# Linear attention, 2048 x 640: value weights in ten transfers instead of fifteen, and a shorter list of final waits

## The chip, the cores and the metric

The kernel runs on one core of a Trainium2 chip. The metric is device time in microseconds (us) for one execution. Before the change three runs took 100.31, 100.75 and 101.52 us; the median is 100.75 us. A separate execution was profiled; its lines are what is read here.

## The reference

One sequence of 2048 rows and 640 features goes through a linear-attention block with 32 heads of width 20, and then through an output projection:

```
qkv = x @ wqkv                      # x: 2048 x 640, wqkv: 640 x 1920
q, k, v = split into 32 heads of 20
phi(t) = where(t > 0, t + 1, exp(t)) + 1e-6
kv  = sum over s of phi(k)[s] (x) v[s]        # 20 x 20 per head
z   = sum over s of phi(k)[s]
o   = (phi(q) @ kv) / (phi(q) . z + 1e-6)
out = o @ wo                        # wo: 640 x 640
```

All inputs and the output are bf16.

## The kernel before, in words

The kernel never forms v. It uses that the sum over rows of phi(k) times v is (phi(k)^T x) times the value part of wqkv. So TensorE first makes phi(k) (`k_half` L288, `k_phi` L302), then P = x^T phi(k), accumulated over 16 row tiles (`state_mm` L316, used by `p_step` L324 and `p_block` L679). From P and the value weights `wv` it makes the small kv blocks (`kv_group` L439, its matmuls are L445), masks them to the heads (`kv_mask` L454), multiplies them with `wo` (`w2_four` L505, `w2_two` L525, whose matmuls are L472) and moves the result into `w2p` by small DMAs (`w2_move`, L494). In between it makes phi(q) transposed (`q_tile` L348, matmuls L354), the denominators (`den` L538, matmuls L544), spreads their reciprocals over the partitions by DMA (`den_spread`, L561) and scales phi(q) with them (`normalize`, L569). Last come the 16 output tiles: `out_mm` (L576) into PSUM, `out_evac` (L599 on ScalarE, L602 on VectorE) into one of four SBUF buffers `osb`, and a store by `out_dma` (L587).

All work is put down in a small plan. `Plan.add` (L36) appends an operation to its engine's list and works out which semaphore values it has to wait for; `Plan.emit` (L78) writes each list out with its waits. The order is written out by hand: the loads first, then a string of letters (L722), one letter per step. Every engine runs its list in order, and so does each DMA queue owner: SyncE (SP) issues nearly all transfers, so a transfer that must wait holds up those behind it.

`Plan.known[eng]` (L30) holds, for each engine, the semaphore values that its list has certainly seen at that point. Each operation carries a `clock`, a copy of what its engine knew when it was added (L69). When an engine waits for an operation, it takes over that operation's clock too (L57 to L59). So an engine can know that a transfer has landed without having waited for that transfer's own semaphore: it is enough that it waited for an operation of another engine which had waited for it. `add` leaves out waits that are already known (L54). The final loop (L730 to L732) does not look at `known`: it makes SP wait for each of the 17 output stores.

The loads stand on SP's queue in this order: part of x and of the key weights (`load_wk`, L235), five transposing loads of x (`load_xT`, L187), and then `load_rest` (L258): the query weights `wqn` (L224), three pieces of x in its own layout `xn` (L230), the value weights `wv` (L266), and `wo` as `wog` (L273, L277). After `load_rest`, SP's list goes on with the two transposes of the z sums (`z_turn`, L423), the moves into `w2p`, the spreading of the reciprocals and the stores.

The value weights are cut into six groups of heads: five of 120 columns and one of 40. In SBUF a 120-column group is stored as two chunks of 60 in slots of 64, with the gaps zeroed by a VectorE memset (L160), for which the first of the `wv` transfers waits. `load_rest` loads them for each of the five 128-row blocks d of wqkv. Groups 0 to 3 are one transfer per block (eight chunks of 60 elements, 120 bytes each, per partition), group 4 another (two chunks of 60) and group 5 a third (one chunk of 40): fifteen transfers. Each transfer has its own semaphore. `kv_group(0)` (letter k in the string) needs groups 0 to 3; `kv_group(1)` (letter K) needs groups 4 and 5.

The output stores use the four `osb` buffers in turn. The evacuation of tile t + 4 writes the buffer that the store of tile t reads, so ScalarE or VectorE waits for that store before it writes. Tiles 0 to 14 have one store each on SP; the last tile has two, one on SP (columns 0 to 479) and one on ScalarE's queue (columns 480 to 639), in `out_last` (L612).

Of the kernel before, what the change touches and what calls it, by code (L numbers as in the profile page):

```python
# [84 lines left out]
def bass_standalone__linear_attn_block__prompt_kernel(nc, x, wqkv, wo, out):  # L85
# [15 lines left out]
    with contextlib.ExitStack() as ctx:  # L101
# [38 lines left out]
        P = Plan(nc, es)  # L140
# [82 lines left out]
        def w_cols(dst, lo, hi, col, key, eng):  # L223
            P.add(eng, lambda e: e.dma_start(  # L224
                dst[:, 0:NC_ * D].rearrange("p (c n) -> p c n", n=D)[:, :, lo:hi],
                wqkv[:, col + lo:col + hi].rearrange("(c p) n -> p c n", p=128)),
                writes=[key], dma=True)

        def load_xn(a, b, eng):
            P.add(eng, lambda e: e.dma_start(  # L230
                xn[:, a * D:b * D].rearrange("p (t n) -> p t n", n=D),
                x[0, 128 * a:128 * b, :].rearrange("(t p) n -> p t n", p=128)),
                writes=[("xn", t) for t in range(a, b)], dma=True)
# [24 lines left out]
        def load_rest():  # L258
            w_cols(wqn, 0, D, 0, "wqn", "sp")
            for a, b in ((2, 8), (8, 12), (12, 16)):  # L260
                load_xn(a, b, "sp")
            for g, n in ((0, 4), (4, 1), (5, 1)):
                f = min(GT, gsz[g])
                k = gsz[g] // f * n
                for d in range(NC_):
                    P.add("sp", lambda e, g=g, f=f, k=k, d=d: e.dma_start(  # L266
                        wv[:, 128 * NG * d:128 * NG * (d + 1)].rearrange(
                            "p (j f) -> p j f", f=64)[:, 2 * g:2 * g + k, 0:f],
                        wqkv[128 * d:128 * (d + 1), 2 * D + goff[g]:2 * D + goff[g] + k * f].rearrange(
                            "p (j f) -> p j f", f=f)),  # L270
                        writes=[("wv", i, d) for i in range(g, g + n)], dma=True)
            for t in range(2):
                P.add("sp", lambda e, t=t: e.dma_start(  # L273
                    wog[64 * t:64 * t + GT, 0:5 * D].rearrange("p (g n) -> p g n", n=D),
                    wo[0:5 * GW, :].rearrange("(g t p) n -> t p g n", t=2, p=GT)[t]),
                    writes=[("wog", g, t) for g in range(5)], dma=True)
            P.add("sp", lambda e: e.dma_start(  # L277
                wog[0:gsz[5], 5 * D:6 * D], wo[goff[5]:, :]),
                writes=[("wog", 5, 0)], dma=True)
# [342 lines left out]
        load_wk()  # L622
        load_xT()
        load_rest()
        warm(5)
        warm(1, 128)
# [102 lines left out]
            P.emit(name, eng)  # L729
        for key in out_keys:  # L730
            op = P.writers[key]
            nc.sync.wait_ge(P.sem_obj[op.sem], op.val)  # L732


# [26 lines left out]
```

## Time and profile before

| what | value |
| --- | --- |
| median of 3 runs | 100.75 us (100.31 to 101.52) |
| the profiled execution's own time | 100.58 us |
| its span, first to last instruction | 99.3 us |
| TensorE matmul busy | 95.1 us, 96% of the span |
| VectorE, ScalarE, GpSimd busy | 63.7, 48.8, 4.7 us |
| granted TensorE clock | 1.000 |
| HBM read and written | 5.90 MB and 2.62 MB |
| issues of `wv` on SP | 15, from 18.5 us to 33.9 us |

How to read it: the span runs from the first to the last instruction that the profiler saw; the execution's own time lies 1.28 us above it. In a group line, "128x320 x170" is the shape and the count, then the busy time in us and the mean of one in ns. "SPq" is the work of SyncE as the issuer of DMAs: the duration of such a row is the time that the issue held SyncE, not the time that the data took; the time to landing is listed apart. A wait line reads "who waited <- whom: us in total, times, longest". In a timeline line the first number is the start, the second the length, both in us.

### The profile page before, as it was taken

Reading aid. Unit: us, or ns where it says so; the run is one execution under the profiler, and the core shown is the slowest. Engines: PE = TensorE matmul, PEld = TensorE weight load, DVE = VectorE, ACT = ScalarE, POOL = GpSimd, SP = SyncE. Lnnn points to the kernel's source line nnn. Section 1 sums busy time; section 2 is a strip of 40 time slices with the busy share of each in tenths; the row PEclk is TensorE's granted clock in tenths of the full one; section 3 lists DMA queues with packets and bytes.
Section 4 is the critical chain, followed back from the end, with each engine's and each line's share of the span. In section 5 each row is a group of like instructions: output and inputs, shape, how many; then the busy total and the mean of one; then the engine's idle time right before and its main releaser. Section 6 shows DMA issues by size and latency. Waiting matters only on the chain.

```text
span 99.3 us, 1827 instructions
## 1 busy us (share of the span) xinstructions
PE 95.1 (96%) x699; PEld 60.8 (61%) x699; DVE 63.7 (64%) x124; ACT 48.8 (49%) x93; POOL 4.7 (5%) x19
## 2 busy tenths in 40 slices
PE   6999999999999999999999999999999999999980
PEld 2457777777755544455678767655556677777760
DVE  5304998898899349989649836759899033551140
ACT  5116455554427020015706648796987665454430
POOL 6400000000000000000000700000000000000000
PEclk9999999999999999999999999999999999999999
DMA  2999989999996169000340023223101257233332
GB/s 60 293 256 245 231 120 119 355 362 361 308 155 91 21 134 196 5 0 0 73 66 7 0 75 99 80 49 88 52 0 51 81 110 240 92 131 132 132 125 77
DMA packets 26448, 12.60 MB, mean 127 GB/s; under 512 B 18632, under 2 KB 26440, under 8 KB 26440
## 3 DMA queue, kind: packets, MB, share of 16 engines
q1 hardware_dynamic: 25720, 11.87, 50.4%
q10 hardware_dynamic: 720, 0.61, 1.9%
q8 instruction: 5, 0.08, 0.3%
q14 instruction: 3, 0.02, 0.1%
HBM read 5.90 MB, written 2.62 MB: 86 GB/s over the span
## 4 chain that ended last, share of the span: by engine, by line
PE 91%; DMA 4%; ACT 1%; ACTq 0%; issue 0%
PE ps L576 22%; PE ps L317 22%; PE ps L354 22%; PE ps L293 22%; DMA wk<-in_wqkv_dram 4%; PE ps L445 1%; PE ps L544 1%; PE ps L472 1%; ACTq L230 0%; ACT L239 0%; ACT osb L599 0%
## 5 line engine op out<-in xcount | busy, mean ns | idle before, releaser
L317 PE MATMUL ps<-pk,xn 128*128 128x480 bf16 (+1 forms) x160 | 23.2, 300 | 0.0
L354 PE MATMUL ps<-xT,wqn 128*128 128x512 bf16 x100 | 23.1, 379 | 0.0
L293 PE MATMUL ps<-wk,xT 128*128 128x320 bf16 x160 | 22.4, 299 | 0.5 <-DMA wk<-in_wqkv_dram 0.2
L576 PE MATMUL ps<-w2p,pq 128*128 128x320 bf16 (+2 forms) x170 | 22.1, 292 | 0.0
L293 PEld LDWEIGHTS ps<-wk,xT 128*128 128x128 bf16 x160 | 15.5, 98 | 7.4 <-DMA wk<-in_wqkv_dram 1.3
L576 PEld LDWEIGHTS ps<-w2p,pq 128*128 128x128 bf16 x170 | 15.9, 98 | 6.3 <-issue 0.2
L317 PEld LDWEIGHTS ps<-pk,xn 128*128 128x128 bf16 x160 | 13.6, 98 | 9.4 <-issue 0.3
L362 ACT ACTIVATE eq<-ps 128x512 bf16<-128x512 f32 x20 | 11.9, 597 | 13.8 <-PE ps L354 13.6
L354 PEld LDWEIGHTS ps<-xT,wqn 128*128 128x128 bf16 x100 | 11.4, 118 | 9.1 <-issue 0.3
L306 ACT ACTIVATE ek<-ps 128x640 bf16<-128x640 f32 x16 | 11.2, 704 | 11.1 <-PE ps L293 10.4
L599 ACT CAST osb<-ps 128x320 bf16<-128x320 f32 (+2 forms) x27 | 11.0, 412 | 9.7 <-PE ps L576 9.0
L311 DVE SCALAR_TENSOR_TENSOR pk<-ps,ek 128x640 bf16<-128x640 f32 x16 | 13.2, 824 | 0.5
L569 DVE TENSOR_TENSOR pq<-pq,rd 128x512 bf16<-128x512 bf16 x20 | 7.3, 418 | 4.3 <-DMA rd<-rdc 4.3
L375 DVE TENSOR_SCALAR eq<-eq 128x512 bf16<-128x512 bf16 x20 | 5.7, 287 | 5.9 <-ACT eq L362 5.8
L602 DVE CAST osb<-ps 128x320 bf16<-128x320 f32 (+1 forms) x7 | 3.2, 457 | 8.7 <-PE ps L576 8.7
L308 DVE TENSOR_SCALAR ek<-ek 128x640 bf16<-128x640 bf16 x16 | 5.2, 324 | 5.4 <-ACT ek L306 5.2
L366 ACT ACTIVATE rq<-ps 128x512 bf16<-128x512 f32 x13 | 7.7, 592 | 0.0
L339 ACT CAST pt<-ps 128x480 bf16<-128x480 f32 x4 | 2.3, 563 | 8.2 <-PE ps L317 8.1
L379 DVE TENSOR_TENSOR pq<-eq,rq 128x512 bf16<-128x512 bf16 x13 | 5.5, 425 | 1.1 <-ACT rq L366 0.7
L388 DVE TENSOR_TENSOR za<-pk 128x1280 f32<-128x1280 bf16 x4 | 5.8, 1483 | 0.0
L382 DVE SCALAR_TENSOR_TENSOR pq<-ps,eq 128x512 bf16<-128x512 f32 x7 | 4.8, 692 | 0.2
L388 DVE TENSOR_TENSOR za<-za 128x1280 f32<-128x1280 f32 x3 | 4.4, 1488 | 0.0
(37 smaller groups left out, 36.2 us busy)
## 6 DMA issues: line engine op xcount, KB each, us to landing
out_dram<-osb SPq DMA_DIRECT2D x15, 160.0 KB, 1.8
xn<-in_x_dram SPq DMA_DIRECT2D x2, 640.0 KB, 8.9
xn<-in_x_dram SPq DMA_DIRECT2D x1, 960.0 KB, 7.1
wqn<-in_wqkv_dram SPq DMA_DIRECT2D x1, 800.0 KB, 5.6
wog<-in_wo_dram SPq DMA_DIRECT2D x2, 375.0 KB, 5.3
w2p<-w2g SPq DMA_DIRECT2D x10, 75.0 KB
wv<-in_wqkv_dram SPq DMA_DIRECT2D x5, 120.0 KB, 5.5
rd<-rdc SPq DMA_DIRECT2D x8, 64.0 KB, 2.2
```

Of the source, the lines that this page charges most:

```text
L293: r = e.matmul(bank(b + h, HALF), xT[:, c * S + 128 * st:c * S + 128 * st + 128], wk[:, c * D + HALF * h:c * D + HALF * (h + 1)], start=(c ...
L306: P.add("act", lambda e: e.activation(fold(t[:, :]), two_banks(b), ACTF.Exp), reads=banks + ["table"], writes=[("ek", st % 3)])
L311: P.add("dve", lambda e: e.scalar_tensor_tensor(fold(pk[:, st * D:(st + 1) * D]), two_banks(b), 0.0, fold(t[:, :]), ALU.max, ALU.add), rea ...
L317: return e.matmul(bank(d // PB[h], PW[h], off=PW[h] * (d % PB[h])), xn[:, st * D + 128 * d:st * D + 128 * d + 128], pk[:, st * D + PO[h]:s ...
L354: r = e.matmul(bank(b), wqn[:, d * D:(d + 1) * D].rearrange("p (q c) -> p c q", c=NC_)[:, c, :], xT[:, d * S + BK * sbk:d * S + BK * (sbk ...
L362: P.add("act", lambda e: e.activation(t[:, :], bank(b), ACTF.Exp), reads=[("bank", b), "table"], writes=[("eq", i)])
L366: P.add("act", lambda e: e.activation(r[:, :], bank(b), ACTF.Relu), reads=[("bank", b), "table"], writes=[("rq", i)])
L375: P.add("dve", lambda e: e.tensor_scalar(t[:, :], t[:, :], 1.0, 1e-6, ALU.min, ALU.add), reads=[("eq", i)], writes=[("eq", i)])
L388: P.add("dve", lambda e: e.tensor_tensor(d_ap, a, b, ALU.add), reads=ra + rb, writes=[dst])
L569: P.add("dve", lambda e: e.tensor_tensor(v, v, rd[i][:, BK * h:BK * (h + 1)], ALU.mult), reads=[("rd", i, 2 * h), ("rd", i, 2 * h + 1), (" ...
L576: r = e.matmul(bank(b, hi - lo), pq[:, c * S + 128 * st:c * S + 128 * st + 128], w2p[:, c * D + lo:c * D + hi], start=(c == 0), stop=(c == ...
L599: P.add("act", lambda e: e.copy(osb[j][:, lo:hi], bank(b, hi - lo)), reads=[("bank", b)], writes=keys)
```

## The change

Two edits. In `load_rest`, groups 0 to 3 and group 4 become one transfer per block, of ten chunks of 60 elements per partition; group 5 stays as it is. In the final loop, a store is skipped when SP's list is already known to have seen it landed.

```
             w_cols(wqn, 0, D, 0, "wqn", "sp")
             for a, b in ((2, 8), (8, 12), (12, 16)):
                 load_xn(a, b, "sp")
-            for g, n in ((0, 4), (4, 1), (5, 1)):
+            for g, n in ((0, 5), (5, 1)):
                 f = min(GT, gsz[g])
                 k = gsz[g] // f * n
                 for d in range(NC_):
...
         for key in out_keys:
             op = P.writers[key]
+            if P.known["sp"].get(op.sem, 0) >= op.val:
+                continue
             nc.sync.wait_ge(P.sem_obj[op.sem], op.val)
```

As built, SyncE issues five transfers fewer. The five big ones have the shape 128x10x60 in place of 128x8x60, and the five of 128x2x60 are gone. At `kv_group(1)` TensorE waits for five DMA semaphores where it waited for ten; at `kv_group(0)` for five, as before. At the end, 5 of the 17 stores are still waited for (tiles 12, 13 and 14 and both of tile 15); a wait instruction takes up to two semaphores, so nine such instructions become three. The rest of each engine's list has the same instructions in the same order.

## Prediction

> **What bounds the kernel now.** I read the page first: how busy each engine is, and the slices.
>
> ```profile
> span 99.3 us, 1827 instructions
> PE 95.1 (96%) x699; PEld 60.8 (61%) x699; DVE 63.7 (64%) x124; ACT 48.8 (49%) x93; POOL 4.7 (5%) x19
> PE   6999999999999999999999999999999999999980
> DMA  2999989999996169000340023223101257233332
> PE 91%; DMA 4%; ACT 1%; ACTq 0%; issue 0%
> ```
>
> TensorE is at 9 in every slice but the first and the last two, and the chain that ended last is TensorE for 91%. The DMA engines are full in the first third and mostly idle after it. Second, the chain in order of time, for where TensorE starts and stops:
>
> ```profile
> 1.72 4.05 DMA wk<-in_wqkv_dram
> 5.82 21.36 PE ps L293 x156
> ...
> 77.26 19.16 PE ps L576 x150
> 96.42 0.02 issue
> 96.44 0.23 ACT osb L599
> ```
>
> From 5.82 to 96.42 us, 90.6 us, every piece of the chain is TensorE. In that stretch a transfer matters only if TensorE would wait for it. The other 8.7 us of the span are the start (key weights, 5.8 us) and the tail after the last matmul (99.3 - 96.4 = 2.9 us). Third, SyncE, which both edits touch, by its timeline and its own waits:
>
> ```profile
> 16.44 2.04 SPq L230 DMA_DIRECT2D xn<-in_x_dram  x3
> 18.52 15.84 SPq L266 DMA_DIRECT2D wv<-in_wqkv_dram  x15
> 34.41 0.92 SPq L273 DMA_DIRECT2D wog<-in_wo_dram  x2
> 35.38 0.37 SPq L277 DMA_DIRECT2D wog<-in_wo_dram  x1
> 47.29 1.32 SPq L423 DMA_TRANSPOSE zt<-zh  x1
> ```
>
> ```profile
> SPq L423 <- DVE zl L415: 12.4, 1, 12.4
> SPq L732 <- DMA out_dram<-osb: 1.6, 1, 1.6
> ```
>
> SyncE is done with the loads at 35.75 us and then has nothing to do until 47.29 us: it waits for VectorE's z sums (the row names zl; the first transpose needs zh). At the very end it waits 1.6 us for a store. Fourth, the two edited lines and the readers of `wv` (matmul L445):
>
> ```profile
> L266 SPq DMA_DIRECT2D wv<-in_wqkv_dram x15: 432/480/3460, 18.5 to 33.9; - x15
> DMA to landing us min/median/max: 1.7/2.8/9.4
> L445 PE MATMUL ps<-pt,wv x30: 179/216/217, 49.7 to 62.8; 128*128 128x120 bf16 x25, 128*128 128x40 bf16 x5
> ```
>
> ```profile
> L732 SPq EVENT_SEMAPHORE  x9: 17/28/28, 97.3 to 99.3; - x9
> ```
>
> The last `wv` transfer is issued at 33.9 us and the slowest takes 9.4 us, so all have landed by 33.9 + 9.4 = 43.3 us at the latest; TensorE first reads `wv` at 49.7 us. The wait instructions of L732 stand between 97.3 and 99.3 us, and 1.6 us of that is the one wait.
>
> **The change part by part.** *The transfers.* Ten issues (five of eight chunks, five of two) become five of ten chunks. Per partition and block that is ten pieces of 120 bytes either way: no byte and no piece less. What goes is five issues. In narrow windows of SyncE's timeline the five eight-chunk issues last 1.72, 3.46, 3.08, 0.58 and 0.94 us (9.78 us); the two-chunk ones 0.70, 0.48 and three times 0.47 us (2.59 us). With the gaps, the ten hold SyncE from 18.52 to 31.32 us, 12.8 us. The trace has no ten-chunk issue, so I bound it: at best each is as short as the cheapest `wv` issue (0.43 us), 2.2 us in all, 10.6 us less than now; at worst each is as long as the longest and grows with its pieces, 3.46 x 10/8 = 4.33 us, 21.6 us in all, 8.8 us more than now. I take 10.2 us, about 2.6 less: equal eight-chunk issues last between 0.58 and 3.46 us, so the length is set by what is still queued ahead and not by their own pieces, and then just the two-chunk ones fall away.
>
> What this does to the end: nothing within these bounds. Behind `wv` on SP's queue stand `wog` and the z transposes. Earlier by 2.6 us, `wog` merely lands earlier and SyncE waits 15 us in place of 12.4 for the z sums. At the worst end the last big issue starts at 18.52 + 4 x 4.33 = 35.8 us; with a landing time also stretched, 9.4 x 10/8 = 11.8 us, it is in at 47.6 us, 2.1 us before L445. `wog` would be issued by 44.2 us and lands within 5.9 us, by 50.1 us, against a first use (L472) at 54.7 us; SyncE is free at 35.75 + 8.8 = 44.6 us, 2.7 us before it is needed. Ahead of `wv` on the same queue stand `wqn` and `xn`; their issues do not move. GpSimd's and ScalarE's queues do not carry `wv`. So 0 at both ends; the cover is TensorE's own 22 us of matmuls from 27.2 to 49.6 us.
>
> [...]
>
> *TensorE's waits.* `kv_group(1)` waits for five semaphores fewer, three wait instructions fewer in TensorE's list. One such instruction lasts 0.05 us at the start of the trace (the start barrier). The chain shows no gap ahead of L445, so they run under the matmuls already queued: 0; if not, at most 3 x 0.05 = 0.15 us of gain. A loss has no source, since none is added.
>
> *The final waits.* Nine wait instructions become three. Eight steps from 97.3 to 99.3 us less the 1.6 us wait leave 0.4 us, 0.05 us each; six fewer save 0.3 us. But they run while the last stores fly: SyncE then reaches the wait for tile 15's store 0.3 us sooner and waits 1.9 us in place of 1.6. After that store has landed, one wait instruction for ScalarE's store follows, as before. So 0; without that cover the whole 0.3 us would be gained. No loss: nothing is queued behind these waits, and nobody waits for SyncE.
>
> Sum: 0 + 0 + 0 against the profiled execution's own 100.58 us, that is 100.6 us, of which 99.3 is span and 1.28 lies around it. That execution is 0.17 us below the median of the three runs (100.75). I put the changed kernel's median between the two, at 100.7 us.
>
> **The rivals.** *A, the tail gives something back (100.1 us).* The final waits are on the path after all, or fewer instructions shift something behind the last matmul: 0.3 us, with TensorE's 0.15 us 0.45, so 100.58 - 0.45 = 100.1. For it: the tail is 2.9 us in which no engine computes. Against it: the 1.6 us wait for the store, longer than the savings.
>
> *B, the shorter load stage is passed on (98.0 us).* If the 2.6 us on SyncE reached the end, 100.58 - 2.6 = 98.0. For it: the DMA engines are at 9 in most slices up to 30 us. Against it: SyncE's 12.4 us idle time behind the loads, and a chain with no DMA after 5.8 us.
>
> *C, slower (102.6 us).* The larger transfers land so late that TensorE stands before L445. [...] From 49.7 us on, every us later is a us on the end. For 2 us the last big transfer must land at 51.7 us, 33.2 us after the first issue; now it is at most 27.53 + 9.4 - 18.52 = 18.4 us, so it would have to take 1.8 times as long. Against it: same pieces and bytes, and even the worst bound lands at 47.6.
>
> *D, the edits do not do what they say.* The list of SyncE has the five transfers and six waits fewer, so they do; only that it shows nowhere is the forecast itself.
>
> **How the numbers follow.** No visible change 0.83; A 0.10; B 0.02; C 0.05. The first has its own range of 100.3 to 101.5 us, the spread of the three runs (0.44 below the median, 0.77 above it), in which the last store's landing, 1.8 us in the median and 2.9 at most, also plays. With A's 100.1 the range is 100.1 to 101.5; it leaves out B, C and a rest of the scatter, under 2 in 10. About 1% (1.0 us) is what a measurement of this kernel can tell from no change. Faster by over 1%: B and a 0.03 share of scatter, 0.05. Slower: C and 0.01 of scatter, 0.06. Within 1%: 0.89.
>
> **What would show it.** Right: ten L266 rows, the loads on SyncE over near 33 us, the wait for zl near 15 us, TensorE's chain still from 5.8 to about 96.4 us without a DMA in it, three L732 rows with a wait of about 1.9 us. Wrong: a DMA piece in the chain after 5.8 us (C), a last matmul clearly before 96 us (B), or a tail shorter than 2.6 us (A). A change of the start, before 5.8 us, or of the 1.28 us around the span would be outside all of these cases.

## The result and the profile after

The changed kernel takes 100.00 us in the median of 22 runs, the kernel before 100.48 us in 22 runs beside it. The ratio is 0.9958, with a 95% interval of 0.994 to 0.9976: faster by 0.4%, less than the 1% named in the prediction as telling a difference from none, but with this many runs clear of 1. Some executions of either kernel take a few per cent longer, and the ratios here and below leave them out, so a ratio is not simply the quotient of two medians. The first three runs of the kernel before (median 100.75 us) had shown it 0.27 us too slow. The profiled execution after took 100.18 us with a span of 98.5 us; before it was 100.58 us with 99.3 us.

The page of the changed kernel, with the lines that answer to those of before:

```profile
span 98.5 us, 1813 instructions
PE 95.4 (97%) x699; PEld 61.1 (62%) x699; DVE 63.7 (65%) x124; ACT 48.8 (50%) x93; POOL 4.7 (5%) x19
...
PE   6999999999999999999999999999999999999991
...
q14 instruction: 2, 0.02, 0.1%
...
PE 93%; DMA 3%; SPq 0%; issue 0%; ACT 0%
```

TensorE's row is the old one up to its last two digits. The q14 line is the queue that the profile calls "instruction" (packets, MB, share); the page of before has three packets there. The chain in the changed kernel, in order of time, its start and its end:

```profile
1.24 3.09 DMA wk<-in_wqkv_dram
4.32 0.05 issue
4.37 0.45 PE ps L293
...
12.16 15.12 PE ps L293 x110
27.27 2.02 PE ps L317 x10
...
77.35 19.16 PE ps L576 x150
96.51 0.02 issue
96.53 0.23 ACT osb L599
```

The chain is at TensorE from 4.37 us, before from 5.82 us, but by 27.2 us it has lost that lead. TensorE ends at 96.51 us, 0.09 us later than before (96.42). So up to there nothing was won; the tail behind the last matmul went from 99.3 - 96.4 = 2.9 us to 98.5 - 96.5 = 2.0 us. SyncE's timeline over the loads, in the changed kernel (start, length, both in us):

```profile
16.85 2.31 SPq L230 DMA_DIRECT2D xn<-in_x_dram  x3
19.21 14.57 SPq L266 DMA_DIRECT2D wv<-in_wqkv_dram  x10
33.83 0.93 SPq L273 DMA_DIRECT2D wog<-in_wo_dram  x2
34.79 0.37 SPq L277 DMA_DIRECT2D wog<-in_wo_dram  x1
47.38 1.22 SPq L423 DMA_TRANSPOSE zt<-zh  x1
```

The loads end at 35.2 us, 0.6 us earlier, and the next transfer still leaves at 47.4 us. What did move is the last tile's store on SyncE. The same narrow window of SyncE's timeline, first of the kernel before:

```profile
96.88 0.33 SPq L587 DMA_DIRECT2D out_dram<-osb  x1
```

and of the changed kernel:

```profile
96.54 0.33 SPq L587 DMA_DIRECT2D out_dram<-osb  x1
```

TensorE ended later and yet the store leaves 0.34 us earlier. The list of transfers of that stretch (95 to 100 us) shows the second difference, the median time from issue to landing in the last column. Before:

```profile
q14 instruction: 1, 0.01, 0.8%
...
out_dram<-osb SPq DMA_DIRECT2D x1, 120.0 KB, 2.3
out_dram<-osb ACTq DMA_DIRECT2D x1, 40.0 KB, 2.2
```

After:

```profile
out_dram<-osb SPq DMA_DIRECT2D x1, 120.0 KB, 1.7
out_dram<-osb ACTq DMA_DIRECT2D x1, 40.0 KB, 1.6
```

Both last stores land 0.6 us sooner after their issue. So two things that the prediction had held fixed were worth almost a microsecond together: a late issue and a slow landing. And one thing went the other way: the execution's own time less its span rose from 1.25 us to 1.70 us (with the span unrounded), so of 0.85 us less in the span only 0.40 us are left in the time.

The records of SyncE around the last store, from the trace of before (start in us, length in us, instruction, line, and the semaphores it waits for):

```
96.403  0.017  EVENT_SEMAPHORE  L81   ScalarE's count
96.884  0.333  DMA_DIRECT2D     L587  VectorE's count       <- the store
97.272  0.017  EVENT_SEMAPHORE  L732
```

The wait in front of the store is over at 96.42 us, and VectorE's count that the store waits for had been reached at 96.24 us. SyncE then does nothing for 0.46 us. In the changed kernel the same two records stand 0.03 us apart. That gap was to be seen before the change, and it was overlooked. A packet of 8192 bytes on q14 passes at 97.51 us before, and at 99.62 us, behind the span, after.

### The profile page after: what moved, and what is told of

Same layout as the page of the kernel before. It is cut to its first block, busy times and chain, and to the rows that moved or that the text cites. A ratio compares the mean times of both kernels' runs of the same rounds, so it can differ in the third digit from the quotient of the medians.

```text
span 98.5 us, 1813 instructions
## 1 busy us (share of the span) xinstructions
PE 95.4 (97%) x699; PEld 61.1 (62%) x699; DVE 63.7 (65%) x124; ACT 48.8 (50%) x93; POOL 4.7 (5%) x19
## 4 chain that ended last, share of the span: by engine, by line
PE 93%; DMA 3%; SPq 0%; issue 0%; ACT 0%
PE ps L293 23%; PE ps L576 22%; PE ps L317 22%; PE ps L354 22%; DMA wk<-in_wqkv_dram 3%; PE ps L445 1%; PE ps L544 1%; PE ps L472 1%; SPq L241 0%; PE ps L200 0%; ACT osb L599 0%
## 5 line engine op out<-in xcount | busy, mean ns | idle before, releaser
L306 ACT ACTIVATE ek<-ps 128x640 bf16<-128x640 f32 x16 | 11.2, 704 | 11.0 <-PE ps L293 10.3
```

The lines of the kernel that those rows point to most:

```text
L306: P.add("act", lambda e: e.activation(fold(t[:, :]), two_banks(b), ACTF.Exp), reads=banks + ["table"], writes=[("ek", st % 3)])
```

## The experiments

Theory F came from this: the gap has a fixed place in SyncE's list. The store was the 80th of SyncE's 89 records before, and it is the 75th of 78 now. F says that SyncE stops for 0.46 us ahead of the 80th record of its list, whichever instruction that is, and that an 8 KB packet on q14 follows (at 97.51 us before, 1.09 us after the stop begins). Two rivals: W, the six wait instructions at the end are what was saved; L, the shorter load stage is passed on to the end. All runs below are compared with the kernel before on the same chip, where its medians were 100.46 to 100.56 us.

**The two parts alone.** `loads_only` keeps all 17 final waits:

```
-            for g, n in ((0, 4), (4, 1), (5, 1)):
+            for g, n in ((0, 5), (5, 1)):
```

F's forecast stands first, then those of W and L:

> Ten transfers of value weights, all 17 final waits kept. [...] Here the store is the 75th, so it leaves within 0.1 us of its wait, and the stop falls among the nine wait instructions behind it, under the store's flight: 0.4 to 0.8 us less than before, ratio 0.992 to 0.996. Theory W (the six final wait instructions are what was saved): nothing, ratio 1.000. Theory L (the shorter load stage is passed on): the whole gain of the change, ratio 0.996, and no stop anywhere.

Measured: 99.61 us, ratio 0.9919 (0.9894 to 0.9943). The store leaves 0.03 us after its wait; the stop, 0.46 us, lies at the 80th record between two final waits. This half of the change is better than the whole, which W excludes, and L had given at most the whole.

`waits_only` has fifteen transfers and the shorter list:

```
             op = P.writers[key]
+            if P.known["sp"].get(op.sem, 0) >= op.val:
+                continue
             nc.sync.wait_ge(P.sem_obj[op.sem], op.val)
```

> Fifteen transfers as before, five of 17 final waits. F: the last tile's store is still the 80th instruction of SyncE's list and still leaves about 0.4 us late; at most the instruction packet no longer falls on the stores' flight: 0 to 0.4 us less than before, ratio 0.996 to 1.000. W: the whole gain, ratio 0.996, with the store leaving on time. L: nothing, ratio 1.000.

Measured: 100.59 us, ratio 1.0014 (0.9987 to 1.0041). The six wait instructions are worth nothing that shows, as predicted, and the store is the 80th record and leaves 0.46 us late. F had allowed a gain if the packet fell behind the flight; it fell on it (97.57 us), and nothing was gained. W is out.

**Adding instructions.** The next kernels put n wait instructions into SyncE's list behind the loads, each for two loads that have landed by then, in the 12 us in which SyncE is idle (as built, the last of them falls together with a wait for VectorE at the end of that time):

```
+    def pad(self, eng, n):
+        op = Op()
+        op.eng, op.fn = eng, None
+        op.waits = [(f"d:{i}", 16) for i in range(2 * n)]
+        self.ops[eng].append(op)
...
+            if op.fn is None:
+                continue
             op.fn(handle).then_inc(self.sem_obj[op.sem], op.inc)
...
         load_rest()
+        P.pad("sp", n)
```

`before_pad6` is the kernel before with n = 6, and nothing else:

> The kernel before, with six more wait instructions on SyncE behind the loads, all for loads that have long landed, in the time in which SyncE is idle. F: the 80th instruction of SyncE is now one of the store of tile 12, which has slack, so the last store leaves on time and the instruction packet is through before it: 0.5 to 0.9 us less than before although work is added, ratio 0.991 to 0.995. W and L: nothing is saved, ratio 1.000 or a little more.

Measured: 99.76 us, ratio 0.993 (0.9908 to 0.9952). Six instructions more make the kernel 0.7% faster. Its tail, from the transfers in the stretch from 95 to 100 us:

```profile
out_dram<-osb SPq DMA_DIRECT2D x1, 120.0 KB, 1.7
out_dram<-osb ACTq DMA_DIRECT2D x1, 40.0 KB, 1.6
```

Fifteen transfers and all final waits, and the stores land as quickly as after the change. Neither W nor L can give that.

`after_pad5` is the changed kernel with n = 5:

> The changed kernel with five such wait instructions behind the loads, so that the last tile's store is the 80th instruction of SyncE's list again. F: the store leaves about 0.4 us late as in the kernel before and the gain is gone or halved: ratio 0.998 to 1.000, the same as with the final waits alone. W and L: both savings are still there, ratio 0.996.

Measured: 100.53 us, ratio 1.0016 (0.9994 to 1.0039). The gain is gone, with both savings still in place:

```profile
out_dram<-osb SPq DMA_DIRECT2D x1, 120.0 KB, 2.3
out_dram<-osb ACTq DMA_DIRECT2D x1, 40.0 KB, 2.2
```

These are the 2.3 and 2.2 us of the kernel before. `loads_pad5` asks what the merged transfers do by themselves: ten transfers, all 17 waits, n = 5.

> Ten transfers, all 17 final waits, and five wait instructions of landed loads behind the loads: SyncE's list is as long as before and the last tile's store is its 80th instruction again. It shows what the merged transfers do by themselves. Theory F: nothing, ratio 0.998 to 1.002, the store leaves 0.4 us late and one engine's share lands about 0.5 us after the others. Theory L: 0.992 to 0.996, as without the five instructions.

Measured: 100.53 us, ratio 1.0001 (0.9969 to 1.0034). The transfers themselves are worth nothing that these runs can tell; L is out. The gain of `loads_only` lies in five instructions fewer ahead of the store.

**Where the stop hurts.** The changed kernel with n = 3, 4, 6 and 8 moves the stop by single instructions.

> The changed kernel with three such wait instructions behind the loads. Theory F, now: SyncE stops for 0.4 to 0.5 us ahead of the 80th instruction of its list, and the 8 KB instruction packet passes 1.0 to 1.2 us after the stop begins, holding up one engine's share of what is in flight by about 0.5 us. Here the 80th instruction is the second of the three final waits: the stop lies under the last store's flight instead of behind the end, the packet at about 98.6 us, when all has landed. 0.3 to 0.5 us less than the changed kernel: ratio to before 0.990 to 0.993. If the stop behind the end in the changed kernel costs nothing: the same as the changed kernel, 0.996.

> The changed kernel with four wait instructions of landed loads: the last tile's store is the 79th instruction of SyncE's list and leaves on time, the stop comes right behind it, at about 96.9 us, and the packet at about 98.0 us, when the stores have nearly landed. Theory F: 99.6 to 99.9 us, ratio 0.990 to 0.994, one instruction away from the run with five, at 1.00. If the packet alone can still hold a share up: one late increment and 0.995 to 0.998.

> The changed kernel with six such wait instructions: the 80th instruction is the wait just ahead of the last tile's store, so the stop lies in the time in which SyncE waits for ScalarE anyway and the store leaves on time, at 96.5 us; the packet (about 97.1 us) falls on the last stores' flight. It parts the two costs. If the packet costs one engine's share about 0.5 us: ratio 0.995 to 0.998. If the late store alone was the cost: 0.990 to 0.993, as with the stop elsewhere. It differs from the run with five such instructions by one instruction, which in itself is work added.

> The changed kernel with eight such wait instructions: the 80th instruction is the wait ahead of the store of tile 14's predecessor, more than 2 us before the last store leaves; the packet is through before the last tile's stores fly. Theory F: neither cost, ratio 0.990 to 0.993, the best of all together with the run with three. Theory W or L would give 0.996 here and in all of these.

Measured: n = 3: 99.82 us, 0.993 (0.9903 to 0.9957). n = 4: 99.88 us, 0.9923 (0.9895 to 0.9952). n = 6: 100.00 us, 0.9935 (0.991 to 0.996). n = 8: 99.74 us, 0.9938 (0.9907 to 0.9968). On either side of n = 5 the time is about 0.7% lower. n = 6 was to part the two costs, and does so only in part: the store left on time, and the packet began at 96.79 us, 0.26 us ahead of the first data of that store (97.05 us), which is the distance of the four slow kernels too (0.27 to 0.28 us). The last shares came a little late (0.11 us for SyncE's store, 0.16 us for ScalarE's), and the time is near what F gave for a late store as the only cost (0.990 to 0.993), though the interval reaches into the other range. In n = 8 the 80th record is the wait ahead of the store of tile 14 itself, 1.5 us before the last store; its ratio lies above the range that F gave, by less than its interval.

Beside n = 4, on the same chip, the changed kernel once more:

> The changed kernel itself, beside the run with four more instructions on the same chip. Theory F with the stop behind the end: 0.3 to 0.5 us slower than that run, its own time 1.6 to 1.7 us above its span where kernels with the stop inside have 1.2 to 1.3. If the stop behind the end costs nothing: as fast as that run.

Measured: 100.26 us, 0.9971 (0.9938 to 1.0004), against 99.88 us for n = 4: 0.38 us slower in the median with four instructions less, over 12 runs each (99.85 to 101.17 us against 99.62 to 100.13). Its instruction queue over the span, and that of n = 4, first the changed kernel:

```profile
span 98.2 us, 1808 instructions
q14 instruction: 2, 0.02, 0.1%
```

n = 4:

```profile
span 98.7 us, 1812 instructions
q14 instruction: 3, 0.02, 0.1%
```

The third packet is inside the span with n = 4 and behind it in the changed kernel, whose own time is 1.67 us above its span against 1.25. That difference is in every run and not only in the profiled ones: 1.63 to 1.74 us in the 34 runs of the changed kernel in its two series, 1.19 to 1.33 us in all runs of the other kernels that list their span. The span alone would have misled here: it is the shorter one of the slower kernel.

All kernels in one table, worked out from SyncE's records in the traces. "Stop begins" is the end of the 79th record, "packet" the start of the last 8 KB packet. In the traces the semaphore of each store is raised 16 times as it lands. One such increment is called a share here, and "one engine's share" in the expectations, though the traces do not name an engine with it; "last share" is how much later the 16th increment of SyncE's last store came than the 15th. The last column but one is the own time less the span. "Hidden" is explained below the table:

| kernel | store is no. | leaves after its wait, us | stop begins, us | packet, us | last share, us | own - span, us | ratio |
| --- | --- | --- | --- | --- | --- | --- | --- |
| before | 80 | 0.46 | 96.42 | 97.51 | 0.46 | 1.25 | 1 |
| `waits_only` | 80 | 0.46 | 96.48 | 97.57 | 0.51 | 1.25 | 1.0014 |
| `after_pad5` | 80 | 0.46 | 96.66 | 97.74 | 0.47 | 1.26 | 1.0016 |
| `loads_pad5` | 80 | 0.46 | 96.69 | 97.78 | 0.28 | 1.26 | 1.0001 |
| after | 75 | 0.03 | behind the end | 99.62 | 0.04 | 1.70 | 0.9958 |
| `after_again` | 75 | 0.03 | behind the end | 99.32 | 0.04 | 1.67 | 0.9971 |
| `loads_only` | 75 | 0.03 | 97.00 | 98.12 | 0.04 | 1.28 | 0.9919 |
| `after_pad3` | 78 | 0.04 | 97.92, hidden | 99.00 | 0.04 | 1.26 | 0.993 |
| `after_pad4` | 79 | 0.04 | 97.06, hidden | 98.18 | 0.03 | 1.25 | 0.9923 |
| `after_pad6` | 81 | 0.06 | 95.66, hidden | 96.79 | 0.11 | 1.25 | 0.9935 |
| `after_pad8` | 83 | 0.04 | 94.55 | 95.74 | 0.04 | 1.28 | 0.9938 |
| `before_pad6` | 86 | 0.03 | 91.82 | 92.91 | 0.06 | 1.25 | 0.993 |

Three groups: the store is the 80th record, ratio 1; the stop is behind the end, 0.996 to 0.997; the stop is anywhere else, 0.992 to 0.994. Whether ten or fifteen transfers, three or nine final wait instructions, plays no part beyond that which these intervals can tell.

The stop itself is to be seen in seven kernels: the 80th record starts 0.46 to 0.47 us after the end of the 79th. In `after_pad8` and `before_pad6` that record is a wait for ScalarE, before which SyncE otherwise idles only 0.35 us. In `after_pad3`, `after_pad4` and `after_pad6` the 80th record is a wait for which SyncE idles just as long without a stop (0.80, 0.59 and 0.49 us); there the place is inferred from the packet alone. So it is behind the end, where no 80th record is in the trace: the packet starts 1.14 us after the last record, in `after` as in `after_again`.

## Why the prediction was right or wrong

**What bounds the kernel: right.** TensorE's chain is the same from 27.2 us to its end, and no load shows in it behind the start. The start differs by 1.4 us (4.37 against 5.82 us), without an effect on the end.

**The transfers: the issues right in size, and no effect of their own.** Five big issues were put at 10.2 us; they last 1.91, 4.29, 2.44, 0.66 and 0.98 us, 10.3 us in all, none above the bound of 4.33. That the length is set by what is still queued ahead was the author's estimate from unequal lengths of equal issues; no run shows what sets it. SyncE is done only 0.6 us earlier and not 2.6, since it came to them 0.7 us later and the five 40-element issues behind them took 3.9 us in place of 2.9. As predicted, none of that reaches the end (`loads_pad5`: 1.0001).

**TensorE's waits and the final waits: right, 0 within the intervals** (TensorE's go with the ten transfers, `loads_pad5`: 1.0001; the final ones, `waits_only`: 1.0014). Three final wait instructions are left, as the text said. SyncE's waits in the changed kernel:

```profile
L734 SPq EVENT_SEMAPHORE  x3: 17/28/28, 97.5 to 98.5; - x3
```

```profile
SPq L423 <- DVE zl L415: 13.1, 1, 13.1
SPq L734 <- DMA out_dram<-osb: 1.4, 2, 0.8
```

The wait for zl is 13.1 us and not near 15, and the longest wait for a store 0.8 us and not about 1.9. In `waits_only`, where the store stays the 80th record, SyncE does wait 1.8 us for it: the cover was read rightly, but not that the store itself would move.

**The step that failed is the sum, "0 + 0 + 0".** Each instruction was costed by its own duration and by the queue behind it. What was not costed is that taking five records out of SyncE's list moves every later one to another place in that list, and one place, the 80th, has a price: the issue and the landing of the last store, which the sum took over "as before", were not fixed. Measured against the start of the last matmul: the store left 96.88 - 96.21 = 0.68 us after its start before, and 96.54 - 96.30 = 0.25 us after the change, 0.43 us sooner. The store's flight, up to its last increment, went from 2.34 to 1.73 us, 0.61 us less; ScalarE's store ended the tail then, at 98.44 us, 0.17 us behind it. That gives 0.43 + 0.61 - 0.17 = 0.87 of the tail's 0.94 us; the rest lies behind the last landing (0.10 us to the end of the span before, 0.04 after). Against it stand the rise of the own time above the span, 1.70 - 1.25 = 0.45 us, and a last matmul 0.09 us later: 0.94 - 0.45 - 0.09 = 0.40 us, by which the profiled times differ.

The prediction had the means to see it. It gave the tail as 2.9 us and the last store's landing as scatter between 1.8 and 2.9 us, but did not ask why a store whose inputs were ready at 96.42 us left at 96.88 us. Its rival A ("fewer instructions shift something behind the last matmul") named the place and the direction, at a chance of 0.10 and with a price of 0.45 us put together from other terms. The tail of 2.0 us is the sign that it had set for A (shorter than 2.6 us), and the move of the own time against the span it had named as outside all of its cases. The time, 100.00 us, lies 0.1 us below the range; of that the base explains more than all, since before has its median at 100.48 and not at 100.75 us. On the right base the range would have held the time, but by luck: neither the tail's 0.9 us nor the 0.45 us against it stood in the sum. The chances (0.89 for within 1%) fit a ratio of 0.9958 for the same reason, that the two half cancel.

**What is shown and what is argued.** Shown: the stop is ahead of the 80th record in all seven kernels in which it is to be seen, and the time follows the place of that record in all of them. In the ten kernels that have an 80th record the 8 KB packet comes 1.08 to 1.19 us after the end of the 79th, wherever that is. Not shown: why SyncE stops there; that the packet belongs to the stop rests on the name of its queue and on that lag. Inferred is that the 0.45 us behind the end are this stop: it rests on the packet 1.14 us after the span. In the kernel before, the stop with what followed it cost about 0.7% of the time (`before_pad6`: 0.993).

Open: how the 0.8 us divide between the late issue and the slow landing. That the packet holds up one share of the stores rests on four kernels in which it begins just before their data (97.5 to 97.8 us) and the last share comes 0.28 to 0.51 us late; in all others it is 0.11 us or less. An estimate from the traces: from the end of the last matmul to the last increment of both stores it is 2.5 to 2.8 us in these four and 1.9 to 2.0 us in the quick kernels other than n = 6; up to the last increment but one of the later store it is 2.2 to 2.4 us in the four. So some 0.3 to 0.5 us would be the last share, and another 0.3 to 0.4 us what delays all shares, the late issue among it. Against the packet as a cost by itself stands n = 6, where it begins as close to the store's data but the store is on time, and the same stretch is 2.1 us. Its packet is over before ScalarE's data begin, though, so whether the packet costs much only beside a late store is not shown.

## What to carry to other kernels

Removing or adding instructions moves all later ones of that engine's list to other places, so an edit that costs nothing where it stands can, as here, move a fixed stop (0.46 us ahead of SyncE's 80th record) onto the last store (`after_pad5`: 1.0016) or off it (`loads_only`: 0.9919). Look at the last store first: compare the end of its last wait with its issue, and its landing with that of the other stores; a gap there (0.46 us, worth about 0.7% with the slow landing behind it) was worth more here than five transfers saved in a covered stage (`loads_pad5`: 1.0001). Before crediting an edit, run it once with harmless instructions that put the list back to its old length; here that took the whole gain away, and harmless instructions alone gave at least as much as the change did (0.993 against 0.9958, with intervals that overlap).

## What the runs showed of the hardware

- SyncE stops for 0.46 to 0.47 us ahead of the 80th record of its list, in all seven kernels in which another wait does not hide it, and an 8 KB instruction packet starts 1.08 to 1.19 us after the stop begins.
- In the changed kernel, with 78 records in SyncE's list, the packet comes 1.14 us behind the span, and the own time is 0.4 us longer against the span (1.67 and 1.70 us above it against 1.25 to 1.28 in the profiled runs). That this is the same stop is inferred.
- The quickest kernels here have the stop inside the program and away from the last store's issue: 99.61 us with `loads_only`, 0.8% less than before and, by the ratios, 0.4% less than the change under study.
